# Late-stage second layers as seven products of halves (Strassen), summed over six experts in PSUM

## The chip, the cores and the metric

One core of a Trainium2 chip runs the whole program. The metric is the device time of one execution in microseconds (us), the median of several runs. Engines are named as in the profile: PE (TensorE matmuls), PEld (its weight loads), DVE (VectorE), ACT (ScalarE), POOL (GpSimd), SP (SyncE, which here only issues DMAs).

## The reference, cut to what matters

Eight batches of eight heads go through attention over a sliding window of 128 positions. Its output, 4608 tokens of 512 features, is the input of a mixture of eight experts. Every token goes through every expert; `P` only weighs the results.

```
x = attention(q, k, v)            # 4608 x 512
logits = x @ w_gate               # 4608 x 8
P = exp(logits - logits.max())
for _ in range(8):                # row and column normalisation in turn
    P /= P.sum(1, keepdims=True) + 1e-09
    P /= P.sum(0, keepdims=True) + 1e-09
    P *= N / E
for e in range(8):
    h = maximum(x @ w1[e], 0)     # 512 -> 1024
    out += P[:, e:e+1] * (h @ w2[e])   # 1024 -> 512
```

## The kernel before, in words

Instructions are issued in the order in which the code names them, and each engine works through its own list in that order. The 4608 tokens are 36 blocks of 128. `xT` holds the transposed attention output of all blocks on chip, in fp16.

**A unit** (`unit_atoms`, L92) is one expert on four blocks (512 tokens). Its first layer is eight atoms `l1`, each four matmuls with 512 moving columns (L103) and a ReLU on ACT that writes `hT` (L110). Its second layer is four atoms `l2`, one for each block, each eight matmuls (L116) that accumulate 128 tokens x 512 features in a PSUM bank. Whenever a weight tile of 128x128 is used, one weight load precedes the matmul. `woven` (L129) alternates the first layer of a unit with the second layer of the unit before.

**Experts 0 and 1** run while attention is going on. Class `Filler` (L148) hands out their atoms, budgeted by two estimates (`L1_US`, `L2_US`), so that PE has work while attention waits for ACT and DVE, and later while DVE does the eight normalisation rounds (L617 to L643). What is left over runs at L644. `P` is not known yet, so `keep` (L480) puts the raw results away: expert 0's into an fp32 accumulator `acc` on chip (L486), expert 1's into an fp16 tile `yo` with three buffers (L489), which `store` sends to the DRAM tensor `ysp` from ACT's queue (L478) when the next result is kept.

**Experts 2 to 7**, the late stage, start when the filler is empty. Expert by expert, the nine units of 512 tokens run, all in `woven`. `add` (L656) lets DVE multiply each result by its column of `P` and add it to `acc` (L667); with expert 2, it first scales expert 0's part (L660) and adds expert 1's from `yb` (L663), which `load_y` brings back. With expert 7 the block is sent out by SP. Weights come by POOL's queue, cast from fp32 to fp16 on the way, into two buffers each (L85, L87): expert e+1's load is issued at the first unit of expert e and waits until the buffer of expert e-1 is free. POOL has nothing else to do after attention.

PSUM has eight banks: two for the scores (`psS`), two buffers `psV` and four buffers `pmm`, which the atoms share. The tiles of attention lie in the pool `asb`, which stays open to the end.

Of the kernel before, what the change touches and what calls it, by code (L numbers as in the profile page):

```python
# [9 lines left out]
FP16 = mybir.dt.float16  # L10
FP32 = mybir.dt.float32
# [3 lines left out]
def kernel(  # L15
# [42 lines left out]
    ident_h = nc.inline_tensor(np.eye(P, dtype=np.float16), name="ident_c")  # L58
    ident32_h = nc.inline_tensor(np.eye(P, dtype=np.float32), name="ident32_c")

    ysp = nc.dram_tensor("ysp", [NBLK, P, HD], FP16, kind="Internal").ap()

    ctx.enter_context(tc.manual_schedule())
    per = ctx.enter_context(tc.tile_pool(name="per", bufs=1))
# [15 lines left out]
    def load_weights(e: int, first: int = 0, last: int = 2):  # L80
# [4 lines left out]
            nc.gpsimd.dma_start(out=w1ts[e], in_=moe_w1[e].rearrange("(dt p) f -> p dt f", p=P))  # L85
        if first <= 1 < last:
            nc.gpsimd.dma_start(out=w2ts[e], in_=moe_w2[e].rearrange("(ft p) d -> p ft d", p=P))  # L87

    acc: dict = {}


    def unit_atoms(e, b0, nb, pool, tag, bufs, finish):  # L92
# [49 lines left out]
            yield 0, a  # L142

    L1_US, L2_US = 0.87, 1.74
    XPE = 3
    CAST_AT = ((0, 1, 2, 3), (1, 2, 3, 4))

    class Filler:  # L148
# [49 lines left out]
                done += got  # L198
            return done

    with (
        tc.tile_pool(name="asb", bufs=1) as asb,
        tc.tile_pool(name="aps", bufs=1, space=bass.MemoryType.PSUM) as aps,
    ):
        mask = asb.tile([P, H, 2 * P], FP16, name="mask")
        rel = asb.tile([P, HD], FP16, name="rel", tag="yo", bufs=3)[:, 0 : 2 * P]

        def make_mask(u):
            for y in range(4 * u, 4 * u + 4):
# [17 lines left out]
            tails[b] = t32  # L227

        def load_qk(b):
            q32 = per.tile([P, H, RI * Dh], FP32, name=f"q32_{b}", tag="a8", bufs=9)  # L230
            k32 = per.tile([P, H, RI * Dh], FP32, name=f"k32_{b}", tag="a8", bufs=9)
            for t, src in ((q32, q), (k32, k)):
                nc.sync.dma_start(
                    out=t, in_=src[b, :, 0:SM, :].rearrange("h (p i) d -> p h (i d)", i=RI)
                )
            raw[b] = (q32, k32)

        def cast_qk(b, j):

            if j == 0:  # L240
                c16s[b] = per.tile([P, 2, RI, H, Dh], FP16, name=f"c16_{b}", tag="a8", bufs=9)
            for n in (1, 0):
                src = raw[b][n][:, 2 * j : 2 * j + 2, :].rearrange("p h (i d) -> p i h d", i=RI)
                to = c16s[b][:, n, :, 2 * j : 2 * j + 2, :]
                if n == 0:
                    nc.vector.tensor_copy(out=to, in_=src)
                else:
                    nc.scalar.copy(out=to, in_=src)  # L248
            if j == NDT - 1:
                raw.pop(b)  # L250
# [6 lines left out]

        def turn_qk(b):
            c16 = c16s.pop(b)
            qk = per.tile([P, 2, RI, NDT, P], FP16, name=f"qk_{b}", tag="a8", bufs=9)  # L260
            for n in range(2):
                nc.sync.dma_start(
                    out=qk[:, n].rearrange("p i j r -> p (i j) r"),
                    in_=c16[:, n].rearrange("p i h d -> p (i h d)"),
                    transpose=True,
                )
            KT[b] = qk
            homes(b)
# [12 lines left out]
            nc.sync.dma_start(out=QKT[b][2], in_=t16, transpose=True)  # L281

        def load_first():
            q32 = per.tile([P, H, RI * Dh], FP32, name="q32_0", tag="a8", bufs=9)
            k32 = per.tile([P, H, RI * Dh], FP32, name="k32_0", tag="a8", bufs=9)
            raw[0] = (q32, k32)
            for j in range(NDT):
                for n in (1, 0):
                    nc.sync.dma_start(
                        out=raw[0][n][:, 2 * j : 2 * j + 2, :],  # L290
                        in_=(q, k)[n][0, 2 * j : 2 * j + 2, 0:SM, :].rearrange(
                            "h (p i) d -> p h (i d)", i=RI
                        ),
                    )
                if j == 1:
                    load_v(0)
            load_v(1)
            load_tail(0)
            load_v(2)
            load_v(3)  # L300
            load_v(4)
            homes(0)
# [101 lines left out]
        def values(b, kb, u):  # L404

            nk, _ = sizes(kb)
            if u == 0:
                xsbs[b, kb] = asb.tile([P, H, Dh], FP16, name=f"xsb_{b}_{kb}", tag="xsb", bufs=3)
            psN = aps.tile([P, 4, Dh + 1], FP32, name=f"psN_{b}_{kb}_{u}", tag="psV", bufs=2)
            ops = []  # L410
            for y in range(2):
                for hb in range(2):
                    hh = 2 * y + hb
                    if kb > 0:
                        ops.append((hh, pts[b, kb - 1, u][:, 2 * hb + y, P : P + nk], vs[b, kb - 1][:, 4 * u + hh, 0 : Dh + 1]))
                    ops.append((hh, pts[b, kb, u][0:nk, 2 * hb + y, 0:nk], vs[b, kb][0:nk, 4 * u + hh, 0 : Dh + 1]))
            if kb == NKB - 1:
                ops = ops[0::2] + ops[1::2]
            for i, (hh, lhsT, rhs) in enumerate(ops):
                nc.tensor.matmul(  # L420
                    out=psN[0:nk, hh, :],
                    lhsT=lhsT,
                    rhs=rhs,
                    start=(i == 0),
                    stop=(i == len(ops) - 1),
                )
            if kb > 0:
                pts.pop((b, kb - 1, u))
            rden = asb.tile([P, 4], FP32, name=f"rden_{b}_{kb}_{u}", tag="rden", bufs=2)
            nc.vector.reciprocal(out=rden[0:nk, :], in_=psN[0:nk, :, Dh])  # L430
            nc.vector.tensor_tensor(  # L431
                out=xsbs[b, kb][0:nk, 4 * u : 4 * u + 4, :],
                in0=psN[0:nk, :, 0:Dh],
                in1=rden[0:nk, :].unsqueeze(2).to_broadcast([nk, 4, Dh]),
                op=ALU.mult,
            )
# [37 lines left out]

        def store():
            while stores:
                blk, yo = stores.pop(0)
                nc.scalar.dma_start(out=ysp[blk], in_=yo)  # L478

        def keep(e, blk, ps):  # L480
            store()
            if e == 0:
                g = blk // 4
                if g not in acc:
                    acc[g] = per.tile([P, 4, HD], FP32, name=f"acc_{g}", tag="a8", bufs=9)
                nc.vector.tensor_copy(out=acc[g][:, blk % 4, :], in_=ps)  # L486
            else:
                yo = asb.tile([P, HD], FP16, name=f"yo_{blk}", tag="yo", bufs=3)
                nc.vector.tensor_copy(out=yo, in_=ps)  # L489
                stores.append((blk, yo))  # L490

        spans = [(0, 2), (2, 2)] + [(4 * g, 4) for g in range(1, NG)]
        order = [(0, 0), (0, 1)]
# [40 lines left out]
        for n, (b, kb, u) in enumerate(steps):  # L534
# [63 lines left out]
            if b < B - 1 and at == (1 if b > 1 else 5) and b:  # L598
                load_tail(b + 1)
        filler.ready = 4 * B  # L600
        filler.fill(1.8)
        gates(4 * B - 4, NBLK)
        filler.ready = NBLK
# [1 line left out]

        nc.vector.tensor_reduce(out=mx_sb[:, 0:1], in_=L_sb, axis=AX.XY, op=ALU.max)
        filler.fill(1.0)
        psM = aps.tile([P, P], FP32, name="psM", tag="psV", bufs=2)
        nc.tensor.transpose(psM[0:1, :], mx_sb[:, 0:1], ident32)
        nc.vector.tensor_reduce(out=mx_sb[0:1, 1:2], in_=psM[0:1, :], axis=AX.X, op=ALU.max, negate=True)  # L610
        filler.fill(1.0)
        psM2 = aps.tile([P, 1], FP32, name="psM2", tag="psV", bufs=2)
        nc.tensor.matmul(out=psM2, lhsT=ones32[0:1, :], rhs=mx_sb[0:1, 1:2])
        nc.vector.tensor_copy(out=mx_sb[:, 2:3], in_=psM2)
        nc.scalar.activation(out=P_sb, in_=L_sb, func=AF.Exp, bias=mx_sb[:, 2:3])
# [1 line left out]
        for it in range(8):  # L617
# [10 lines left out]
                out=cs_sb, in_=P_sb.rearrange("p c e -> p e c"), axis=AX.X, op=ALU.add  # L628
            )
            filler.fill(2.9)  # L630
            psC = aps.tile([P, E], FP32, name=f"psC_{it}", tag="psV", bufs=2)
            nc.tensor.matmul(out=psC, lhsT=ones32, rhs=cs_sb)  # L632
            nc.vector.tensor_scalar(out=ca_sb, in0=psC, scalar1=1e-9, scalar2=None, op0=ALU.add)
            nc.vector.reciprocal(out=ca_sb, in_=ca_sb)
# [6 lines left out]
                op1=ALU.mult,  # L641
            )
            filler.fill(0.8)  # L643
        while filler.fill(5.0):  # L644
            pass
        store()
        load_weights(2)


        yb: dict = {}  # L650

        def load_y(g):
            yb[g] = asb.tile([P, 4, HD], FP16, name=f"yb_{g}", tag=("qN", "kN")[g % 2], bufs=2)
            nc.sync.dma_start(out=yb[g], in_=ysp[4 * g : 4 * g + 4].rearrange("m p d -> p m d"))

        def add(e, blk, ps):  # L656
            g = blk // 4
            a = acc[g][:, blk % 4, :]
            if e == 2:
                nc.vector.tensor_scalar(  # L660
                    out=a, in0=a, scalar1=P_sb[:, blk, 0:1], scalar2=None, op0=ALU.mult
                )
                nc.vector.scalar_tensor_tensor(  # L663
                    out=a, in0=yb[g][:, blk % 4, :], scalar=P_sb[:, blk, 1:2], in1=a,
                    op0=ALU.mult, op1=ALU.add,
                )
            nc.vector.scalar_tensor_tensor(  # L667
                out=a, in0=ps, scalar=P_sb[:, blk, e : e + 1], in1=a, op0=ALU.mult, op1=ALU.add
            )
            if e == E - 1:  # L670
                if blk < 4 * B:
                    t0 = S * (blk // 4) + P * (blk % 4)
                    nc.sync.dma_start(out=out[t0 : t0 + P, :], in_=a)
# [2 lines left out]
                        t0 = S * (2 * (blk - 4 * B) + half) + SM  # L676
                        nc.sync.dma_start(out=out[t0 : t0 + TL, :], in_=a[TL * half : TL * half + TL])

        def late():
            for e in range(2, E):  # L680
                for g in range(NG):
                    if g == 0 and e + 1 < E:
                        load_weights(e + 1)
                    if e == 2:
                        load_y(g)
                    yield 0, unit_atoms(e, 4 * g, 4, aps, ("pmm", "pmm"), (4, 4), add)

        for _, atom in woven(late()):
            atom()


# [28 lines left out]
```

## Time and profile before

| what | us |
|---|---|
| median of 3 runs (lowest, highest) | 1109.33 (1108.95, 1110.06) |
| the profiled execution, whole | 1111.33 |
| its span, first to last instruction | 1109.1 |
| PE busy in the span | 1079.8 |
| DVE, ACT, POOL busy | 404.7, 437.4, 70.2 |
| late stage, first matmul to last (354.0 to 1104.4) | 750.4 |

The mean granted TensorE clock is 0.996 of full speed. A group line of the page names source line, engine, operation, the tiles written and read, the shape and the count; after the bar stand the busy time and the mean duration of one, then the idle time of the engine just before these instructions with what ended it. Durations of matmuls overlap, so the pace is read from start to start. A timeline line gives the start, the time until the group's end, engine, line, operation and count, and in brackets the idle time before it. `POOLq`, `ACTq` and `SPq` lines are the issue of DMAs.

### The profile page before, as it was taken

Reading aid. Unit: us, or ns where it says so; the run is one execution under the profiler, and the core shown is the slowest. Engines: PE = TensorE matmul, PEld = TensorE weight load, DVE = VectorE, ACT = ScalarE, POOL = GpSimd, SP = SyncE. Lnnn points to the kernel's source line nnn. Section 1 sums busy time; section 2 is a strip of 40 time slices with the busy share of each in tenths; the row PEclk is TensorE's granted clock in tenths of the full one; section 3 lists DMA queues with packets and bytes.
Section 4 is the critical chain, followed back from the end, with each engine's and each line's share of the span. In section 5 each row is a group of like instructions: output and inputs, shape, how many; then the busy total and the mean of one; then the engine's idle time right before and its main releaser. Section 6 shows DMA issues by size and latency. Waiting matters only on the chain.

```text
span 1109.1 us, 14385 instructions
## 1 busy us (share of the span) xinstructions
PE 1079.8 (97%) x5963; PEld 505.1 (46%) x5963; DVE 404.7 (36%) x755; ACT 437.4 (39%) x729; POOL 70.2 (6%) x126
## 2 busy tenths in 40 slices
PE   5899999999999999999999999999999999999998
PEld 3564444444444444444444444444444444444443
DVE  4555666565482455542222222222222222222222
ACT  5566555555332433333333333333333333333332
POOL 2112133230000000000000000000000000000000
PEclk9999999999999999999999999999999999999999
DMA  9995598951326211040002200040002200001113
GB/s 205 199 239 139 110 194 172 191 122 41 108 41 123 47 39 38 1 76 1 1 1 38 38 1 1 1 77 1 1 1 38 38 1 1 1 20 76 77 76 95
DMA packets 127280, 73.90 MB, mean 67 GB/s; under 512 B 84464, under 2 KB 118512, under 8 KB 127216
## 3 DMA queue, kind: packets, MB, share of 16 engines
q1 hardware_dynamic: 108528, 51.33, 18.8%
q0 software_dynamic: 13072, 16.79, 9.6%
q10 hardware_dynamic: 5616, 4.88, 1.6%
q8 instruction: 46, 0.75, 0.3%
q14 instruction: 18, 0.15, 0.0%
HBM read 66.76 MB, written 14.16 MB: 73 GB/s over the span
## 4 chain that ended last, share of the span: by engine, by line
PE 84%; DVE 1%; DMA 1%; issue 0%; DVEq 0%
PE psh L103 41%; PE psy L116 41%; PE psN L420 1%; PE psS L372 1%; DMA ysp<-yo 1%; PE psG L464 0%; DVE acc L486 0%; DVE cs_sb L627 0%; PE psC L632 0%; DVE L_sb L621 0%; DVE yo L489 0%; DVE rs_sb L618 0%; DVE rs_sb L620 0%; DVE L_sb L635 0%; DVE acc L667 0%
## 5 line engine op out<-in xcount | busy, mean ns | idle before, releaser
L110 ACT ACTIVATE hT<-psh 128x512 f16<-128x512 f32 (+1 forms) x592 | 345.4, 586 | 576.4 <-PE psh L103 563.7
L103 PE MATMUL psh<-xT,w1t 128*128 128x512 f16 (+1 forms) x2368 | 554.8, 376 | 2.7 <-DVE yo L489 2.4
L116 PE MATMUL psy<-w2t,hT 128*128 128x512 f16 x2304 | 542.6, 379 | 0.0
L667 DVE SCALAR_TENSOR_TENSOR acc<-psy,L_sb,acc 128x512 f32<-128x512 f32 x216 | 162.2, 751 | 541.3 <-PE psy L116 541.3
L103 PEld LDWEIGHTS <-w1t 128*128 128x128 f16 x2368 | 226.8, 99 | 255.9 <-issue 9.1
L116 PEld LDWEIGHTS <-hT 128*128 128x128 f16 x2304 | 222.2, 98 | 264.8 <-issue 3.0
L385 ACT ACTIVATE pt<-psS 128x1024 f16<-128x1024 f32 (+2 forms) x80 | 68.0, 850 | 64.3 <-PE psS L372 41.5
L398 DVE TENSOR_TENSOR pt<-pt,mask 128x1024 f16<-128x1024 f16 (+2 forms) x80 | 53.2, 666 | 42.1 <-ACT pt L385 41.8
L489 DVE CAST yo<-psy 128x512 f16<-128x512 f32 x36 | 24.9, 691 | 47.7 <-PE psy L116 41.1
L420 PEld LDWEIGHTS <-pt 128*128 128x128 f16 (+2 forms) x576 | 29.2, 103 | 23.0 <-issue 7.2
L85 POOL DMA_DIRECT2D w1t<-in_moe_w_dram x8 | 6.1, 767 | 520.6 <-PE psh L103 520.6
L486 DVE COPY acc<-psy 128x512 f32<-128x512 f32 x36 | 24.8, 690 | 36.7 <-PE psy L116 36.6
L346 POOL CAST v<-v 128x512 f16<-128x512 f32 (+1 forms) x40 | 28.9, 723 | 128.1 <-DMA v<-in_v_dram 92.9
L420 PE MATMUL psN<-v,pt 128*128 128x65 f16 (+2 forms) x576 | 34.8, 199 | 0.9 <-DVE pt L398 0.7
L431 DVE TENSOR_TENSOR xsb<-psN,rden 128x256 f16<-128x256 f32 (+1 forms) x80 | 33.8, 423 | 3.0
L372 PE MATMUL psS<-qN,kN 64*128 64x256 f16 (+1 forms) x256 | 25.9, 274 | 3.9 <-ACT pt L385 3.0
L663 DVE SCALAR_TENSOR_TENSOR acc<-yb,L_sb,acc 128x512 f32<-128x512 f16 x36 | 27.0, 751 | 1.3
L273 POOL COPY kN<-qk 128x512 f16<-128x512 f16 x20 | 22.8, 1183 | 68.2 <-DMA qk<-c 68.2
L248 ACT CAST c<-k 128x512 f16<-128x512 f32 x32 | 19.5, 615 | 9.6 <-DMA k<-in_k_dram 3.8
L372 PEld LDWEIGHTS <-kN 64*128 64x128 f16 x256 | 9.2, 95 | 21.7 <-issue 19.4
L313 PE MATMUL psT<-ident,c 128*128 128x128 f16 x96 | 9.0, 249 | 10.1 <-ACT c L248 9.7
L660 DVE TENSOR_SCALAR acc<-acc,L_sb 128x512 f32<-128x512 f32 x36 | 17.2, 477 | 0.0
(48 smaller groups left out, 161.7 us busy)
## 6 DMA issues: line engine op xcount, KB each, us to landing
v<-in_v_dram SPq DMA_DIRECT2D x32, 256.0 KB, 4.1
w1t<-in_moe_w_dram POOLq DMA_DIRECT2D x8, 1024.0 KB, 8.2
w2t<-in_moe_w_dram POOLq DMA_DIRECT2D x8, 1024.0 KB, 9.1
out_dram<-acc SPq DMA_DIRECT2D x32, 256.0 KB, 2.0
q<-in_q_dram SPq DMA_DIRECT2D x7, 1024.0 KB, 7.0
k<-in_k_dram SPq DMA_DIRECT2D x7, 1024.0 KB, 8.9
ysp<-yo ACTq DMA_DIRECT2D x36, 128.0 KB, 2.1
yb<-ysp SPq DMA_DIRECT2D x9, 512.0 KB, 4.0
```

What stands on the lines that cost most here:

```text
L103: nc.tensor.matmul(out=ps[:, 0:nt], lhsT=w1ts[e][:, dt, P * ft : P * ft + P], rhs=xT[:, b0 : b0 + nb, dt, :], start=(dt == 0), stop=(dt == ...
L110: nc.scalar.activation(out=st["hT"][:, ft, 0:nt], in_=ps[:, 0:nt], func=AF.Relu)
L116: nc.tensor.matmul(out=ps, lhsT=st["hT"][:, ft, P * ms : P * ms + P], rhs=w2ts[e][:, ft, :], start=(ft == 0), stop=(ft == NFT - 1),)
L346: nc.gpsimd.tensor_copy(out=vt[0:nk, :, 0:Dh], in_=v32s.pop((b, kb))[0:nk])
L372: nc.tensor.matmul(out=ps[0:nk, hb, y, 0:n], lhsT=cols(b, 1, j, hb, kb), rhs=cols(b, 0, j, hb, kb, 1 + both),)
L385: nc.scalar.activation(out=pt[0:nk, :, 0 : nk + nn], in_=ps[0:nk, :, :, 0 : nk + nn].rearrange("p a y n -> p (a y) n"), func=AF.Exp, scale ...
L398: nc.vector.tensor_tensor(out=pt[0:nk, :, 0:w], in0=pt[0:nk, :, 0:w], in1=mask[0:nk, hs, 0:w], op=ALU.mult)
L420: nc.tensor.matmul(out=psN[0:nk, hh, :], lhsT=lhsT, rhs=rhs, start=(i == 0), stop=(i == len(ops) - 1),)
L431: nc.vector.tensor_tensor(out=xsbs[b, kb][0:nk, 4 * u : 4 * u + 4, :], in0=psN[0:nk, :, 0:Dh], in1=rden[0:nk, :].unsqueeze(2).to_broadcast ...
L489: nc.vector.tensor_copy(out=yo, in_=ps)
L663: nc.vector.scalar_tensor_tensor(out=a, in0=yb[g][:, blk % 4, :], scalar=P_sb[:, blk, 1:2], in1=a, op0=ALU.mult, op1=ALU.add,)
L667: nc.vector.scalar_tensor_tensor(out=a, in0=ps, scalar=P_sb[:, blk, e : e + 1], in1=a, op0=ALU.mult, op1=ALU.add)
```

## The change

The late stage is rewritten; attention and the first two experts' matmuls are as before.

1. Expert 0's results go to `ysp` too, as fp16, like expert 1's. `acc` of all tokens is gone.
2. After attention the pool `asb` is closed. In its place a pool `lp` holds experts 2 to 6: first-layer weights, the four quarters of the second-layer weights, and five sums or differences of quarters for each (`sums_of`), made by POOL. Expert 7 uses the old weight buffers. Each is loaded once, experts 2 to 6 in five DMAs each (before: two).
3. After the normalisation `P` is transposed by PE, written to DRAM (`ptd`) and read back for each unit, spread over all partitions (`load_p`).
4. A late unit is now 256 tokens and one expert; the order is token group by token group (18), in each the six experts. DVE multiplies `xT` by `P` ahead of the first layer (`make_x`): `P` is positive, so it may go through the ReLU.
5. The second layer has 256 tokens in two halves of 128, 1024 hidden in two halves, 512 features in two halves. Instead of eight products of halves there are seven, each four matmuls of 256 moving columns, from sums of halves of `h` (`make_sums`, DVE) and of weights. All seven are summed over the six experts in PSUM (three and a half banks), and `gather` combines them once per group into `acc`, which `begin` has filled with experts 0 and 1.

The core of the diff:

```diff
+        first_pool.close()
...
+        def load_last(e):
...
+            if e < E - 1:
+                W1L[e] = lp.tile([P, NDT, Fd], FP16, name=f"w1l_{e}")
+                bd = lp.tile([P, 2, NF2, HB], FP16, name=f"w2d_{e}")
+                st = lp.tile([P, 2, NF2, HB], FP16, name=f"w2s_{e}", tag="s4", bufs=2)
...
+                nc.gpsimd.dma_start(out=W1L[e], in_=w1src)
+                for to, (a, c) in ((q11, (0, 0)), (q12, (0, 1)), (q21, (1, 0)), (q22, (1, 1))):
+                    nc.gpsimd.dma_start(out=to, in_=src[a, c])
...
+        def sums_of(e, f6, f7, f4, f3, f1):
...
+                nc.gpsimd.tensor_tensor(out=to, in0=q[x], in1=q[y], op=op)
...
+        load_last(2)
+        load_last(3)
+        for e in range(2, E - 1):
+            sum_last(e)
+            if e + 2 < E - 1:
+                load_last(e + 2)
...
+        PT = 12
+        for c in range(NBLK // PT):
...
+            store()
+            pt_sb = per.tile([P, 2 * P], FP32, name=f"pt_sb_{c}", tag="yo", bufs=YO)
+            nc.vector.tensor_copy(out=pt_sb[0 : PT * E, 0:P], in_=psP[0 : PT * E, 0:P])
+            nc.sync.dma_start(
...
+            filler.fill(0.8)
...
+        units = [(g, e) for g in range(NBLK // 2) for e in range(2, E)]
...
+        def make_x(n):
...
+            nc.vector.tensor_tensor(
+                out=xs(n).rearrange("p (d b t) -> p d b t", d=NDT, b=2),
+                in0=xT[:, 2 * g : 2 * g + 2].rearrange("p b d t -> p d b t"),
+                in1=pbc.pop(n).unsqueeze(1).to_broadcast([P, NDT, 2, P]),
+                op=ALU.mult,
+            )
...
+        def l1_bank(n, i):
...
+            for f in range(2):
+                ft = 2 * i + f
+                for dt in range(NDT):
+                    nc.tensor.matmul(
...
+            nc.scalar.activation(out=h[n][:, 2 * i : 2 * i + 2, :], in_=ps, func=AF.Relu)
...
+        def product(n, m):
...
+            for f in range(NF2):
+                nc.tensor.matmul(
+                    out=Ms[g, bank][:, half, :],
+                    lhsT=left(n, m, f),
+                    rhs=W2L[e][RIGHT[m]][:, f, :],
...
+        store()
+        for n in range(2):
+            load_p(n)
+        filler.fill(3.0)
+        for n in range(2):
+            make_x(n)
+        while filler.fill(5.0):
+            pass
+        store()
+        load_last(E - 1)
+        sum_last(E - 1)
...
+        pairs = ((3, 4), (5, 2), (6, 7), (1,))
+        late: list = []
+        for n in range(len(units) + 1):
+            last = n > 0 and units[n - 1][1] == E - 1
+            if n > 0:
+                make_sums(n - 1)
+            for g, m in late:
+                gather(g, m)
...
+            if n > 0:
+                make_x(n + 1)
+                load_p(n + YO)
...
+            for i in range(4):
+                if n < len(units):
+                    l1_bank(n, i)
+                if n > 0:
+                    for m in pairs[i]:
+                        product(n - 1, m)
+                if last and i in (1, 2):
+                    for m in pairs[i - 1]:
+                        gather(units[n - 1][0], m)
```

`make_sums` is three DVE operations on fp16: two of 1024 elements a partition (sums over the hidden halves, differences over the token halves) and one of 512. `gather` is three DVE operations of 512 and six of 256 elements a group, each with a PSUM operand. `begin` is four operations of 512. The tag `yo` (three buffers) now serves the stored results of both experts, the transposed `P` and the tiles of `load_p`.

## The prediction

> **What bounds the kernel now.** I read the page's busy shares and chain first, then the groups by shape, then the timeline around the two places the change touches.
>
> ```profile
> PE 1079.8 (97%) x5963; PEld 505.1 (46%) x5963; DVE 404.7 (36%) x755; ACT 437.4 (39%) x729; POOL 70.2 (6%) x126
> ...
> PE psh L103 41%; PE psy L116 41%; PE psN L420 1%; PE psS L372 1%; DMA ysp<-yo 1%; PE psG L464 0%; DVE acc L486 0%; DVE cs_sb L627 0%; PE psC L632 0%; DVE L_sb L621 0%; DVE yo L489 0%; DVE rs_sb L618 0%; DVE rs_sb L620 0%; DVE L_sb L635 0%; DVE acc L667 0%
> ```
>
> The chain that ended last is expert matmuls (82%). The windows view shows how pure the late stage is:
>
> ```profile
> 366.00:700.00 334.00, 334.00 (x1550) 151.41 (x1548) 112.14 (x166) 115.85 (x194) 3.27 (x4) 1.00 0.11 21
> 700.00:1100.00 400.00, 400.00 (x1855) 181.38 (x1854) 87.86 (x117) 137.34 (x230) 3.27 (x4) 1.00 0.12 32
> ```
>
> Columns: stretch, length, then PE, PEld, DVE, ACT, POOL busy with counts, clock, DMA. PE never pauses, at 334/1550 = 215.5 ns per matmul of 512 columns; DVE is at 22 to 34%, POOL idle. Only fewer PE columns can shorten this stage. It lasts from 354.0 to the last matmul's end at 1104.4: 750.4 us, of which 3456 x 215.6 ns = 745.1 is pace and about 5 a stall at 357 to 362, shown below.
>
> **What the change takes away.** A unit of 256 tokens has 32 first-layer matmuls and 7 x 4 = 28 second-layer ones, each of 256 columns with a weight load of its own; 108 units make 6480. Before, the same work is 64 such halves. The price of the new shape is in the trace, from the first units of two blocks:
>
> ```profile
> 39.88 3.67 PE L103 MATMUL psh<-xT,w1t 128*128 128x256 f16 x32
> 43.39 3.62 PE L116 MATMUL psy<-w2t,hT 128*128 128x512 f16 x16
> ```
>
> 32 matmuls of 256 columns take 43.39 - 39.88 = 3.51 us, 109.7 ns each, though each has a weight load (98 ns median): the load still hides. 6480 x 109.7 = 710.8 us, so the stage loses 750.4 - 710.8 = **39.6 us**. Ends: half of 216 ns (108.0) gives 50.6; 112 ns gives 24.6.
>
> **Does the new stage keep PE fed?** One unit is 60 x 109.7 = 6.58 us. ACT: four ReLUs of 512 elements at 597 ns, 2.4 us. DVE: fp16 products of 1024 elements from SBUF (L398) take 0.68 us, 768 take 0.56, so `make_sums` is 0.68 + 0.68 + about 0.42 = 1.8; `make_x` of 1024 elements with an fp32 operand lies between 2 x 0.48 (L660, 512) and 2 x 0.75 (L663), I take the latter, 1.5, as L663 too has two operands of two types. `begin`: 2 x (0.48 + 0.75) = 2.5. `gather`: 3 x 0.75 (L667) + 6 x 0.42 (L431, 256) = 4.8. A group of six units costs DVE 6 x 3.3 + 2.5 + 4.8 = 27 us of 39.5. It must also be in time: the last ReLU of a unit ends some 0.4 us into the next, the sums by 2.2; the products that need them come 2.6, 4.4 and 6.1 us in. At a group's turn, the gathers of products 5 and 2 end near 0.4 us into the next unit and free the scores' banks, which are wanted at 0.9. If the sums ran at one element per cycle (twice 0.68), the gathers would be some 1.5 us later and PE would wait about 1 us at each of 18 turns. I take 0; end 18.
> SP issues 108 reads of `P`, three units (20 us) ahead; 128 KB stores land in 1.7 to 8.5 us, so they are early.
>
> **What the change adds at the start of the stage: the term that decides.** POOL must load and add for experts 2 to 6 after attention gives its memory back (last mask use 286.4, last transpose of `xsb` about 294; I take 290), and all six experts are wanted within the first six units, where before expert 3 was wanted 125 us after expert 2. The parts:
> - An issue by POOL is 0.75 us (L85). Ten for experts 2 and 3: 7.7.
> - 1 MB lands 8.2 to 9.1 us after issue, and two back to back move at about 205 GB/s, 5.1 us each. Expert 2 is there near 303.
> - An add of 1024 fp16 elements by POOL is not in the trace. A POOL cast of 512 takes 0.61 us (L346 median), a strided copy of 512 takes 1.07 (L273 median). Ends: 1.2 (1024 at the cast's rate) and 4.3 (two operands at the copy's rate). I take 2.4, two operands at the cast's rate, the plain-stride row being the nearer.
> - POOL and DVE hold each other up. These are DVE's and POOL's timelines:
>
> ```profile
> 171.33 0.98 DVE L398 TENSOR_TENSOR pt<-pt,mask 128x768 f16<-128x768 f16 x1 [0.65 <-ACT pt L385]
> ...
> 174.28 1.41 DVE L398 TENSOR_TENSOR pt<-pt,mask 128x768 f16<-128x768 f16 x1 [0.43 <-ACT pt L385]
> ...
> 276.20 0.56 DVE L398 TENSOR_TENSOR pt<-pt,mask 128x768 f16<-128x768 f16 x1 [0.66 <-ACT pt L385]
> ```
>
> ```profile
> 170.81 4.46 POOL L273 COPY kN<-qk 128x512 f16<-128x512 f16 x4 [10.73 <-DMA qk<-c]
> ```
>
> The same product takes 0.56 us alone and up to 1.41 under POOL's copies; POOL's copies stretch from 1.07 to 1.44 at most. So I put 0.5 us on each add: 2.9.
> Chain: 303 + 25 adds x 2.9 (72.5) + 15 issues x 0.77 (11.6) = 387. Expert 7's two loads are issued behind them and land at 402; its five adds end at 417. PE, without stalls, would begin the stage at 354, want expert 7's first layer at 354 + 5 x 6.58 = 387, its sums from 394, and finish that step at 400. It finishes at about 418: **18 us late**. Each 0.1 us on an add moves this by 3 us.
> PE's own way there has little slack left, so part is paid twice over, by two things. DVE's two-operand work in the normalisation rounds (L621, L635, 0.46 each) and in the first units waits behind adds. And the stores, twice as many, share the DMA engines with weight loads:
>
> ```profile
> 349.79 8.55 DMA ysp<-yo
> 358.33 0.03 issue
> 358.36 0.05 DVEq L489
> 358.41 0.04 issue
> 358.45 0.70 DVE yo L489
> 359.16 0.04 issue
> 359.20 7.89 PE psh L103 x28
> ```
>
> This is the chain view: beside one weight load a store takes 8.5 us (1.7 without), DVE's cast behind it waits for the buffer, ACT's queue waits for DVE with its ReLUs, and PE stops 2.4 us. Some 20 results leave in 287 to 354, and weights now move through all of it. With a result each 3.4 us and three buffers, 10.3 us cover 0.7 + 2 + 6, mostly. I give these together 13 us of PE's time ahead of the stage, covered by the 18, and **3 us** beyond it; ends 0 and 15. The way of `P` through DRAM (two landings of 2 to 8.5 us against about 10 us of filler) lies under the same cover.
>
> [...]
>
> **The end.** Behind the last matmul stood one 0.75 us step and the output. Now `gather` of the last group stands behind the last sums, 4.8 us of which about 3.6 come after PE: **+3 us**.
>
> **Sum.** 1109.1 - 39.6 + 18 + 3 + 3 = 1093.5 of span. The profiled execution took 2.2 us more than its span; the median of the runs, 1109.33, is 0.2 above the span, so the median after is forecast as **1094 us**.
>
> **The rivals.**
> - *The start is hidden* (adds at 1.2 to 2.2 us, or stores that don't bite): 1109.3 - 39.6 + 3 gives 1073, with a few us of stall 1080. For it: 60 us of filler lie between attention and the stage. Against: 25 adds and 15 loads in it. Chance 0.22.
> - *Slower: POOL's chain.* Same place, an add of 4.3 us: 30 x 1.4 = 42 us more, 1136. It decides from the point where the losses reach 39.6, an add of about 3.4 us with its waits. [...] Against: the operands here run in plain stride. Chance 0.17.
> - *PE stalls at every group's turn* because DVE is late: +18, or sums at half rate, about 1104 to 1112. Against: 12 us of slack a group. Chance 0.08.
> - *The shape does not pay*: a weight load per 109.7 ns could slip when both operands change source; at 116 ns the stage is as long as before. Against: the row of 32. Chance 0.03.
> - My forecast, 1084 to 1105: 0.50.
>
> The range leaves out the ends of the first two: 1072 to 1118. A measurement of this kernel can tell about 0.2% (2 us) from no change. Faster 0.77: forecast, hidden start, half of the late turns; within 0.2%: 0.05; slower 0.18.
>
> **What will show it.** Right: 60 matmuls per 6.6 us after about 420 us with PE full; idle PE between 330 and 420, ended by POOL's sums or expert 7's load; adds of 2.4 to 3 us. Wrong: idle PE in the later groups, ended by DVE, which would put the loss at 18 turns; a pace above 112 ns; or adds near 1.2 us, and then no idle time at 387.

## The result and the profile after

The changed kernel takes 1125.97 us (median of 4 runs, 1124.32 to 1126.65), the kernel before, measured beside it, 1109.32 (1108.95 to 1110.06): a ratio of 1.0147, 95% interval 1.0129 to 1.0165. It is slower by 1.5%, where 1094 was forecast. The profiled execution took 1126.23 us, its span is 1124.5, against 1109.1 before: **15.4 us** to account for.

The page after, busy shares and the chain that ended last:

```profile
PE 1052.0 (94%) x8990; PEld 805.5 (72%) x8990; DVE 653.7 (58%) x1136; ACT 437.8 (39%) x729; POOL 145.6 (13%) x171
...
PE 79%; DVE 5%; issue 1%; ACT 0%; DVEq 0%
```

PE has 27.8 us less to do, and the span grew all the same: PE's share fell from 97% to 94%, and 5% of the chain is now VectorE. The windows view says where. The first stretch runs from the end of attention to the start of the late stage, the other two lie in the late stage:

```profile
308.50:404.00 95.50, 67.26 (x311) 30.52 (x310) 71.37 (x89) 19.01 (x32) 72.47 (x51) 0.86 0.89 148
440.00:700.00 260.00, 260.00 (x2385) 233.03 (x2383) 150.91 (x244) 94.69 (x159) 0.00 (x0) 1.00 0.17 50
700.00:1100.00 400.00, 400.00 (x3667) 358.54 (x3665) 234.49 (x379) 145.90 (x245) 0.00 (x0) 1.00 0.16 47
```

The late stage is what the change promised: full, at 260/2385 = 109.0 ns per matmul of 256 columns, with VectorE at 58% and nothing lost at the groups' turns. The loss lies in front of it. By stage:

| stretch | before, us | after, us | difference |
|---|---|---|---|
| start to the last gate matmuls (end of attention) | 294.05 | 308.5 | +14.4 |
| from there to the first late matmul (354.04; 404.01) | 60.0 | 95.5 | +35.5 |
| late stage to its last matmul | 750.4 | 711.9 | -38.5 |
| after the last matmul | 4.7 | 8.6 | +3.9 |

**The second row: the normalisation rounds.** VectorE's timeline inside one long wait and after it:

```profile
352.06 0.47 DVE L685 SCALAR_TENSOR_TENSOR L_sb<-L_sb,ca_sb 128x288 f32<-128x288 f32 x1
352.56 0.45 DVE L668 TENSOR_REDUCE rs_sb<-L_sb 128x36 f32<-128x288 f32 x1
353.05 8.36 DVE L669 TENSOR_SCALAR rs_sb<-rs_sb 128x36 f32<-128x36 f32 x1
361.44 0.38 DVE L670 RECIPROCAL rs_sb<-rs_sb 128x36 f32<-128x36 f32 x1
361.85 1.90 DVE L671 TENSOR_TENSOR L_sb<-L_sb,rs_sb 128x288 f32<-128x288 f32 x1
```

and POOL's in the same time:

```profile
352.97 2.18 POOL L633 TENSOR_TENSOR w2f<-w2s,w2d 128x1024 f16<-128x1024 f16 x1
355.05 4.24 POOL L633 TENSOR_TENSOR w2f<-w2d,w2s 128x1024 f16<-128x1024 f16 x2
359.21 2.15 POOL L633 TENSOR_TENSOR w2f<-w2s,w2d 128x1024 f16<-128x1024 f16 x1
361.28 2.14 POOL L633 TENSOR_TENSOR w2f<-w2d 128x1024 f16<-128x1024 f16 x1
```

A step of 36 elements a partition, which takes 0.18 us in other rounds, is on record as *busy* for 8.36: it began 0.08 us after the first of five adds and ended when the fourth did. L671 (0.46 alone) then waits out the fifth. The record calls this time busy and not idle, so the waits view does not show it; it shows in durations only. PE sees the end of it:

```profile
350.99 0.59 PE L682 MATMUL psC<-cs_sb,ones 128*128 128x8 f32 x2 [8.35 <-DVE cs_sb L677]
364.50 0.60 PE L682 MATMUL psC<-cs_sb,ones 128*128 128x8 f32 x2 [7.98 <-DVE cs_sb L677]
378.60 0.60 PE L682 MATMUL psC<-cs_sb,ones 128*128 128x8 f32 x2 [8.49 <-DVE cs_sb L677]
```

A handy measure of the rounds, used for every run below, is the time from the first to the last weight load of the column-sum matmuls (L682; L632 before): 63.1 us (315.7 to 378.8), against 29.1 before (301.5 to 330.6). These are the lines, before and after:

```profile
L632 PEld LDWEIGHTS psC<-cs_sb,ones x16: 186/189/190, 301.5 to 330.6; 128*128 128x128 f32 x16
```

```profile
L682 PEld LDWEIGHTS psC<-cs_sb,ones x16: 186/238/333, 315.7 to 378.8; 128*128 128x128 f32 x16
```

In the whole stretch from 308.5 to 404.0 PE is idle for 28.2 us (before, from 294 to 354: 0.9). The other 8 us of the 35.5 are PE being busy longer, 67.3 us against 59.1 for about the same number of matmuls (311 and 309); the granted clock is 0.86 there, against 1.00.

**The first row: a pause at 47 us.** Windows of before, then of after (length, PE, PEld, DVE, ACT, POOL, clock, DMA share, GB/s):

```profile
47.00:58.00 11.00, 7.48 (x84) 5.20 (x81) 8.59 (x19) 7.11 (x10) 1.39 (x3) 0.90 0.98 166
58.00:72.00 14.00, 14.00 (x163) 9.95 (x160) 7.82 (x20) 8.91 (x20) 2.98 (x10) 0.96 1.01 268
```

```profile
47.00:58.00 11.00, 0.38 (x4) 0.31 (x4) 1.87 (x5) 1.50 (x3) 1.32 (x4) 0.67 1.04 189
58.00:72.00 14.00, 11.60 (x89) 7.62 (x89) 7.06 (x16) 7.87 (x13) 1.32 (x4) 0.53 1.03 276
```

PE stands for 11 us, and the granted clock is 0.53 in the 14 us behind. The DMA engines were full in both kernels (share 0.98 to 1.04). ACT's timeline names the odd thing:

```profile
55.83 0.33 ACTq L478 DMA_DIRECT2D ysp<-yo  x1
56.50 1.14 ACT L247 CAST c<-k 128x512 f16<-128x512 f32 x2 [12.37 <-DMA v<-in_v_dram]
```

ACT casts keys, but is released by a load of *values*, which it does not use. Ahead of the cast in its queue stands a store of expert 0's result, which the kernel before did not have. The trace names a completion counter for every DMA. Those that SP and ACT issue share eight (99, 101 to 105, 107 and 108; POOL's have 110 to 117), and after the first use of each, all 372 of them here were issued only when the last DMA with the same counter had landed. Expert 0's third store has the same one (99) as a load of values that SP issued at 43.86; that load lands at 55.75, beside expert 1's weights, and ACT issues the store at 55.83. That was the suspicion; the experiments test it.

**The small rest.** Expert 7's sums hold VectorE once more (L768 took 2.60 us, L737 3.13; the medians are 0.68 and 1.22), and PE once:

```profile
429.81 1.87 PE L753 MATMUL psh<-aux,w1l 128*128 128x256 f16 x8 [2.49 <-DVE aux L737]
```

and the last gathers, 2.73 and 1.54 us, end 3.2 us behind the last matmul instead of a step of 0.75.

### The profile page after: what moved, and what is told of

Same layout as the page of the kernel before. It is cut to its first block, busy times and chain, and to the rows that moved or that the text cites. A ratio compares the mean times of both kernels' runs of the same rounds, so it can differ in the third digit from the quotient of the medians.

```text
span 1124.5 us, 21205 instructions
## 1 busy us (share of the span) xinstructions
PE 1052.0 (94%) x8990; PEld 805.5 (72%) x8990; DVE 653.7 (58%) x1136; ACT 437.8 (39%) x729; POOL 145.6 (13%) x171
## 4 chain that ended last, share of the span: by engine, by line
PE 79%; DVE 5%; issue 1%; ACT 0%; DVEq 0%
PE psh L753 33%; PE psS_m L808 17%; PE psV_m L808 12%; PE psh L102 7%; PE psy L115 7%; DVE rs_sb L669 2%; PE psN L420 1%; PE psS L371 1%; DVE L_sb L671 1%; DVE acc L854 0%; DVE aux L737 0%; DVE L_sb L685 0%; DVE cs_sb L677 0%; PE psC L682 0%; DVE yo L483 0%
## 5 line engine op out<-in xcount | busy, mean ns | idle before, releaser
L760 ACT ACTIVATE hs<-psh 128x512 f16<-128x512 f32 x432 | 257.9, 597 | 457.1 <-PE psh L753 370.1
L753 PE MATMUL psh<-aux,w1l 128*128 128x256 f16 x2880 | 373.4, 273 | 2.5 <-DVE aux L737 2.5
L753 PEld LDWEIGHTS <-w1l 128*128 128x128 f16 x2880 | 282.1, 98 | 35.9 <-issue 2.7
L808 PEld LDWEIGHTS <-hs 128*128 128x128 f16 x2592 | 254.0, 98 | 30.1 <-DVE hs L765 0.4
L765 DVE TENSOR_TENSOR hs<-hs 128x1024 f16<-128x1024 f16 x108 | 74.9, 694 | 284.7 <-ACT hs L760 284.7
L102 PE MATMUL psh<-xT,w1t 128*128 128x512 f16 (+1 forms) x640 | 151.1, 375 | 0.4 <-ACT hT L109 0.3
L115 PE MATMUL psy<-w2t,hT 128*128 128x512 f16 x576 | 136.4, 382 | 0.0
L109 ACT ACTIVATE hT<-psh 128x512 f16<-128x512 f32 (+1 forms) x160 | 87.8, 555 | 121.2 <-PE psh L102 100.8
L737 DVE TENSOR_TENSOR aux<-xT,pbc 128x1024 f16<-128x1024 f16 x108 | 133.3, 1235 | 0.0
L115 PEld LDWEIGHTS <-hT 128*128 128x128 f16 x576 | 53.7, 99 | 62.4 <-issue 5.9
L102 PEld LDWEIGHTS <-w1t 128*128 128x128 f16 x640 | 58.9, 103 | 51.5 <-issue 10.6
L768 DVE TENSOR_TENSOR hs<-hs 128x1024 f16<-128x1024 f16 x108 | 75.9, 703 | 0.0
## 6 DMA issues: line engine op xcount, KB each, us to landing
k<-in_k_dram SPq DMA_DIRECT2D x7, 1024.0 KB, 10.3
```

The lines of the kernel that those rows point to most:

```text
L102: nc.tensor.matmul(out=ps[:, 0:nt], lhsT=w1ts[e][:, dt, P * ft : P * ft + P], rhs=xT[:, b0 : b0 + nb, dt, :], start=(dt == 0), stop=(dt == ...
L109: nc.scalar.activation(out=st["hT"][:, ft, 0:nt], in_=ps[:, 0:nt], func=AF.Relu)
L115: nc.tensor.matmul(out=ps, lhsT=st["hT"][:, ft, P * ms : P * ms + P], rhs=w2ts[e][:, ft, :], start=(ft == 0), stop=(ft == NFT - 1),)
L737: nc.vector.tensor_tensor(out=xs(n).rearrange("p (d b t) -> p d b t", d=NDT, b=2), in0=xT[:, 2 * g : 2 * g + 2].rearrange("p b d t -> p d ...
L753: nc.tensor.matmul(out=ps[:, f, :], lhsT=W1L[e][:, dt, P * ft : P * ft + P], rhs=xs(n)[:, HB * dt : HB * dt + HB], start=(dt == 0), stop=( ...
L760: nc.scalar.activation(out=h[n][:, 2 * i : 2 * i + 2, :], in_=ps, func=AF.Relu)
```

## The experiments

Ratios are to the kernel before, with 95% intervals.

| run | us | ratio | rounds, us |
|---|---|---|---|
| after | 1125.97 | 1.0147 [1.0129, 1.0165] | 63.1 |
| no_adds | 1092.62 | 0.9859 [0.9845, 0.9874] | 29.2 |
| before_adds | 1125.77 | 1.0159 [1.0144, 1.0174] | 43.2 |
| half_adds | 1137.9 | 1.0265 [1.0248, 1.0282] | 63.7 |
| gap_memset | 1126.64 | 1.0163 [1.0146, 1.018] | 63.4 |
| gap_dma | 1143.75 | 1.0315 [1.0298, 1.0331] | 82.2 |
| rounds_psum | 1100.75 | 0.9929 [0.9911, 0.9946] | 28.4 |
| dve_adds | 1092.04 | 0.9855 [0.984, 0.9869] | 29.2 |
| pool_store | 1133.41 | 1.0225 [1.021, 1.0241] | 63.5 |
| qk2_one_later | 1125.12 | 1.0152 [1.0137, 1.0167] | 62.9 |
| qk2_two_later | 1114.85 | 1.0057 [1.004, 1.0074] | 62.5 |
| dve_adds_qk2 | 1081.13 | 0.9761 [0.9738, 0.9783] | 29.1 |
| rounds_psum_qk2 | 1090.17 | 0.9843 [0.9817, 0.9869] | 28.4 |

### Are the adds the cause of the slow rounds?

Two causes are set against each other: VectorE's steps wait for POOL's adds (called the lock theory), or the loads and stores slow the stretch (traffic).

**no_adds**: the loads stay, the sums on POOL go.

```diff
-                nc.gpsimd.tensor_tensor(out=to, in0=q[x], in1=q[y], op=op)
...
+            q.update(f1=q["q11"], f3=q["q22"], f4=q["q11"], f6=q["q22"], f7=q["q11"])
```

> The 30 adds of weight quarters are left out (the products read quarters in place of sums), so part of the computation is missing; loads, stores and everything else stay. Lock theory: the eight normalisation rounds shrink from 66 us to about 35, because DVE's two-operand steps no longer wait for POOL; the late stage starts near 370 instead of 404 and has no pause near 429. Time 1083 to 1090 us. Traffic theory (the weight loads and the doubled stores slow the stretch, not the adds): the rounds stay above 55 us, time 1115 to 1126.

Measured: 1092.62 us; the rounds are back at 29.2 us with all loads beside them. Not the whole way to the 1083 to 1090 expected, since PE pauses in front of the late stage, where stores run beside weight loads:

```profile
358.71 1.13 PE L102 MATMUL psh<-xT,w1t 128*128 128x512 f16 x4 [4.18 <-DVE yo L483]
364.68 3.61 PE L102 MATMUL psh<-xT,w1t 128*128 128x512 f16 x16 [1.52 <-DVE yo L483]
```

The pause at 47 us is as in the kernel after: it has nothing to do with the adds.

**before_adds**: the kernel before, with 25 adds of the same size on POOL, on scratch tiles, and no other DMA.

```diff
         filler.ready = 4 * B
+        for n in range(25):
+            pt = asb.tile([P, 4, 2 * P], FP16, name=f"scratch_{n}", tag="pt", bufs=4)
+            nc.gpsimd.tensor_tensor(out=pt, in0=mask[:, 0:4, :], in1=mask[:, 4:8, :], op=ALU.add)
```

> The kernel before, with 25 POOL adds of 1024 fp16 elements on scratch data put in after attention, without any new DMA; the result is not touched. Lock theory: the adds alone stretch the normalisation rounds by 20 to 32 us, time 1129 to 1142 us. Traffic theory: nothing reads or writes the adds' data, POOL is idle there and no transfer is added, so 1109 to 1111.

Measured: 1125.77 us, 17.5 more than before. So adds alone slow the rounds, to 43.2 us, and the time. But it is 3.2 us below the range expected, and each wait is here of one add at most, though 25 stand back to back:

```profile
299.42 1.71 DVE L622 TENSOR_SCALAR rs_sb<-rs_sb 128x36 f32<-128x36 f32 x1
...
312.39 2.13 DVE L638 SCALAR_TENSOR_TENSOR L_sb<-L_sb,ca_sb 128x288 f32<-128x288 f32 x1
```

### How long does VectorE wait?

**half_adds**: each add is made as two of half the size.

```diff
-                nc.gpsimd.tensor_tensor(out=to, in0=q[x], in1=q[y], op=op)
+                for lo in range(0, NF2, 2):
+                    nc.gpsimd.tensor_tensor(
+                        out=to[:, lo : lo + 2], in0=q[x][:, lo : lo + 2], in1=q[y][:, lo : lo + 2], op=op
+                    )
```

> Each POOL add is cut into two of 512 elements: the same work in twice as many instructions. If DVE is kept out for a number of POOL instructions (four in the trace, 8.4 us), its long waits halve to some 4.3 us and the rounds shorten by 10 to 15 us: time 1110 to 1117. If it is kept out until POOL has nothing ready, the long waits stay near 8.4 us or more and the time is 1124 to 1132. If each instruction were a fair turn, waits would be at most 1.2 us and the time near 1100.

Measured: 1137.9, more than any theory had. Adds of 1.1 us, and still VectorE waits like this:

```profile
354.05 9.39 DVE L674 TENSOR_TENSOR L_sb<-L_sb,rs_sb 128x288 f32<-128x288 f32 x1
```

Eight half adds long, as long as four whole ones before. It is not a number of instructions that VectorE waits for. The rounds took 63.7 us as in after; the 12 us more lie just behind the part that this measures, at the adds of the last expert, where VectorE's last step of the rounds waited for all ten half adds and PE stood idle 10.48 us for it:

```profile
380.32 11.67 DVE L688 SCALAR_TENSOR_TENSOR L_sb<-L_sb,ca_sb 128x288 f32<-128x288 f32 x1
```

**gap_memset** and **gap_dma**: something else between the adds, a small fill or one of the loads that stood behind them. In gap_dma the four loads of quarters are also issued in another order.

```diff
                 nc.gpsimd.tensor_tensor(out=to, in0=q[x], in1=q[y], op=op)
+                if e < E - 1:
+                    nc.gpsimd.memset(gap, 0.0)
```

```diff
-            sum_last(e)
-            if e + 2 < E - 1:
-                load_last(e + 2)
+            sum_last(e, load_last(e + 2, False) if e + 2 < E - 1 else ())
...
                 nc.gpsimd.tensor_tensor(out=to, in0=q[x], in1=q[y], op=op)
+                if between:
+                    between.pop(0)()
```

> The kernel after, with a fill of 128x2 elements on GpSimd behind each sum, which reads no tile. [...]

> The kernel after, with the loads of the expert two later issued one by one between the sums on GpSimd, instead of five loads behind five sums. VectorE was let in before the fifth sum in every case so far where loads followed it. Theory that only back-to-back sums shut VectorE out: its long waits shrink from 8.4 us to one sum (about 2.2 us) or two, the rounds take 40 to 52 us instead of 66, and the time falls by 12 to 24 us, to 1102 to 1114. [...]

Measured: 1126.64 and 1143.75. Fills change nothing (1125.97 in after); the longest waits are 6.16, 8.24 and 8.25 us. With the loads in between it got worse, not better: waits of 6.31, 6.04 and 6.66 us through two adds and the loads between them, and then one of 24.55. VectorE's and POOL's timelines of gap_dma:

```profile
361.42 24.55 DVE L675 TENSOR_TENSOR L_sb<-L_sb,rs_sb 128x288 f32<-128x288 f32 x1
```

```profile
362.02 2.13 POOL L637 TENSOR_TENSOR w2f<-w2d 128x1024 f16<-128x1024 f16 x1
364.08 0.79 POOL L615 DMA_DIRECT2D w2s<-in_moe_w_dram  x1
364.89 2.13 POOL L637 TENSOR_TENSOR w2f<-w2s,w2d 128x1024 f16<-128x1024 f16 x1
...
383.54 2.10 POOL L637 TENSOR_TENSOR w2f<-w2d 128x1024 f16<-128x1024 f16 x1
```

One step of 0.46 us stood through eleven adds. By the record it began 0.6 us ahead of the first of them, while POOL issued a load, and the 0.8 us in which POOL issued the next one (364.08) did not let it in either. What does end such a wait stays open: between one add (before_adds) and eleven (gap_dma) everything was seen.

### Which steps of VectorE wait?

Over all these runs the steps of the rounds that wait are L669, L671 and L685 by the lines of after (0.18, 0.46 and 0.46 us alone; up to 8.38 in after, 24.55 in gap_dma and 11.67 in half_adds), and in the late stage the fp16 sums and products (up to 2.60 and 3.13 in after); never a reduction (0.43 to 0.68 us in the rounds), a reciprocal (0.20 and 0.38), or a step that reads PSUM (L683, also a scaling by a constant, takes 0.15 to 0.17 us throughout). All that waited read SBUF alone, with two tensors, or scale SBUF to SBUF.

**rounds_psum**: the matrix of the rounds and its row sums lie in PSUM, the adds stay on POOL. (The column sums' PSUM tile moves to another pool to make room.)

```diff
+        R = aps.tile([P, GT], FP32, name="psR", tag="psV", bufs=2)
+        Pr = R[:, 0 : NBLK * E].rearrange("p (c e) -> p c e", e=E)
+        rs = R[:, 320 : 320 + NBLK]
...
-            nc.vector.tensor_scalar(out=rs_sb, in0=rs_sb, scalar1=1e-9, scalar2=None, op0=ALU.add)
+            nc.vector.tensor_scalar(out=rs_sb, in0=rs, scalar1=1e-9, scalar2=None, op0=ALU.add)
...
-                out=P_sb,
-                in0=P_sb,
+                out=Pr,
+                in0=Pr,
```

> The kernel after, with the matrix of the normalisation rounds held in PSUM instead of SBUF: VectorE's three steps that were seen to wait (scaling the row sums, and the two products with the broadcast sums) read their first operand from PSUM. GpSimd's sums stay where they are. In all runs so far only these steps waited, while reductions, reciprocals and the copies out of PSUM never did. Theory that a step waits only if both of its tensor operands, or its source and target, are in SBUF: the waits vanish, the rounds take 30 to 38 us instead of 66, the late stage starts some 30 us earlier, and the time is 1092 to 1100 us. Rival, any two-operand step of VectorE waits for GpSimd's sums wherever its operands are: the waits of 8 us stay and the time is 1120 to 1130.

Measured: 1100.75 us, a hair above the range, and no step of the rounds waits, beside the same adds (POOL adds from 339.02 to 349.4 in this run):

```profile
342.25 0.47 DVE L688 SCALAR_TENSOR_TENSOR psR<-psR,ca_sb 128x288 f32<-128x288 f32 x1
...
343.25 0.20 DVE L672 TENSOR_SCALAR rs_sb<-psR 128x36 f32<-128x36 f32 x1
...
343.89 0.47 DVE L674 TENSOR_TENSOR psR<-psR,rs_sb 128x288 f32<-128x288 f32 x1
...
345.84 0.46 DVE L688 SCALAR_TENSOR_TENSOR L_sb<-psR,ca_sb 128x288 f32<-128x288 f32 x1
```

The place of the operand that is read decided here: L672 and the last L688 write to SBUF and did not wait either (0.20 and 0.46 us). The rest to 1092 is PE waiting 3.13 and 2.53 us for stores' buffers before the late stage, and 2.53 and 2.40 us for products of VectorE behind the adds of experts 6 and 7.

**dve_adds**: VectorE makes the sums itself, experts 2 and 3 after the rounds, 4 before the late loop, 5 to 7 in its first steps.

```diff
-                nc.gpsimd.tensor_tensor(out=to, in0=q[x], in1=q[y], op=op)
+                nc.vector.tensor_tensor(out=to, in0=q[x], in1=q[y], op=op)
...
-        for e in range(2, E - 1):
-            sum_last(e)
-            if e + 2 < E - 1:
-                load_last(e + 2)
...
+        for e in (2, 3):
+            sum_last(e)
+            load_last(e + 2)
+            filler.fill(0.8)
```

> The kernel after, with all sums of weights on VectorE: experts 2 and 3 after the normalisation, expert 4 before the late loop, 5 to 7 within its first steps; the loads stay on GpSimd's queue and in the same number. Lock theory: without a two-operand operation on GpSimd the rounds take 34 to 38 us as in no_adds, the late stage starts at 370 to 385, some 5 to 10 us of sums come onto VectorE's path, and the time is 1090 to 1103 us. Rival, the loads themselves slow the rounds, or VectorE's sums are as dear as GpSimd's (2.2 us each, 66 us in all on the path of the late stage's first steps): 1115 or more.

Measured: 1092.04 us, rounds 29.2, first late matmul at 371.9. An add costs VectorE 0.68 us, a third of POOL's 2.1 (timeline of dve_adds_qk2, below):

```profile
340.37 0.68 DVE L633 TENSOR_TENSOR w2f<-w2s,w2d 128x1024 f16<-128x1024 f16 x1
340.97 1.28 DVE L633 TENSOR_TENSOR w2f<-w2d,w2s 128x1024 f16<-128x1024 f16 x2
```

### What is the pause at 47 us?

**pool_store**: the first four of expert 0's stores from POOL's queue, whose DMAs have other counters than those eight (110 to 117 in after).

```diff
-                nc.scalar.dma_start(out=ysp[e, blk], in_=yo)
+                (nc.gpsimd if e == 0 and blk < 4 else nc.scalar).dma_start(out=ysp[e, blk], in_=yo)
```

> The first four stores of expert 0 are issued by POOL instead of ACT. Theory: in the changed kernel ACT's third store waits 11 us for a completion counter that it shares with a load of v, and ACT's copies and so PE wait behind it (47 to 58 us); with the stores off ACT's queue that pause goes, and attention ends about 13 us earlier, time 1110 to 1115 us. Rival: the pause is the DMA engines, full with expert 1's weights and the next loads; then it stays or moves, time 1122 to 1127.

A miss: 1133.41 us, and the pause is longer. The timelines of POOL and PE:

```profile
55.60 0.61 POOL L345 CAST v<-v 128x512 f16<-128x512 f32 x1 [11.66 <-DMA v<-in_v_dram]
...
57.46 1.66 POOL L478 DMA_DIRECT2D ysp<-yo  x3
```

```profile
64.39 1.44 PE L312 MATMUL psT<-ident,c 128*128 128x128 f16 x12 [16.55 <-DVE yo L483]
```

In POOL's queue the stores stood behind casts of those same values. The move exchanged one wait for the load by another and says nothing for or against the counter.

**qk2_one_later** and **qk2_two_later**: the loads of batch 2's queries and keys, which number two among the eight, are issued later. The first leaves the third store on the counter of the late load, the second puts it on that of a load of values that landed at 39.56.

```diff
-            if (b, at) == (0, 7):
+            if (b, at) == (1, 0):
                 load_qk(2)
```

```diff
-            if (b, at) == (0, 7):
+            if (b, at) == (1, 1):
                 load_qk(2)
```

> The kernel after, with the load of batch 2's queries and keys issued three steps of attention later (at the first step of batch 1 instead of step 7 of batch 0). In the program this leaves the completion counter of expert 0's third store as it is: the counter of the load of values that lands at 55.8 us. It is the control for qk2_two_later. Counter theory: the pause of TensorE between 47 and 58 us stays, and the time is 1123 to 1128 us. Rival, traffic: the third store and the loads of values are late because the load of the queries and keys shares the DMA engines with expert 1's weights; with it moved away the pause shrinks, and the time falls by 5 to 14 us, to 1112 to 1121.

> The same load one step later still (second step of batch 1). Expert 0's third store now shares its completion counter with a load of values two earlier, which landed at about 40 us, before the store is wanted. Nothing else differs from qk2_one_later but one step's place of two loads. Counter theory: the pause between 47 and 58 us is gone (at most 3 us of it left), attention ends near 296 us instead of 308, and the time falls by 10 to 14 us, to 1111 to 1116. Rival, traffic: as qk2_one_later, within 3 us. The rounds of the normalisation, with GpSimd's sums beside them, keep their 66 us in both theories.

Measured: 1125.12 and 1114.85 us. One step's place of two loads is worth 10.3 us. PE in the windows of the one and of the other:

```profile
47.00:58.00 11.00, 0.00 (x0) 0.10 (x1) 1.39 (x3) 1.11 (x3) 1.07 (x3) 0.62 1.08 193
```

```profile
47.00:58.00 11.00, 7.82 (x80) 5.22 (x79) 7.73 (x18) 7.26 (x11) 1.12 (x2) 0.80 1.09 197
58.00:72.00 14.00, 14.00 (x155) 9.57 (x153) 7.00 (x18) 7.82 (x18) 3.01 (x9) 0.91 0.95 277
```

DMA is as full in both (share 1.08 and 1.09). And the load of values on counter 99 lands no earlier in qk2_two_later, at 56.37 (55.75 in after, 56.13 in qk2_one_later). But there the third store has another counter, and ACT's queue goes on without it:

```profile
45.14 0.33 ACTq L478 DMA_DIRECT2D ysp<-yo  x1
45.82 1.14 ACT L247 CAST c<-k 128x512 f16<-128x512 f32 x2 [2.05 <-DVE c L245]
```

So it was the counter, not the traffic. The last gate matmul starts at 298.0, 3.0 later than before (295.0), 11.3 earlier than after (309.3). What makes the 3.0 stays open.

### Both repairs

**dve_adds_qk2** and **rounds_psum_qk2** join the second move with each cure of the rounds.

> Both repairs together: sums on VectorE and the load of batch 2's queries and keys at the second step of batch 1. If the two losses are separate (the startup's pause by the counter, the slow rounds by GpSimd's sums), the gains add: dve_adds less 10 to 14 us, that is 1078 to 1092 us, under the kernel before. Rival: the pause's time comes back as a later wait (weights not landed when the late stage starts), and the time is that of dve_adds less at most 4.

> The rounds in PSUM and the load of batch 2's queries and keys at the second step of batch 1. If the two gains add, rounds_psum less 10 to 12 us, 1081 to 1090; against dve_adds_qk2 (1081) it has no sums on VectorE but the pause at expert 7's sums (some 3 us). If the rounds still wait: 1109 to 1117.

Measured: 1081.13 and 1090.17 us. The gains add (1092.04 - 10.9; 1100.75 - 10.6), the second with 0.2 us over the range expected. The first beats the kernel before by 2.4%:

```profile
PE 1041.9 (96%) x8990; PEld 799.1 (74%) x8990; DVE 631.6 (58%) x1166; ACT 436.4 (40%) x729; POOL 81.0 (7%) x141
```

Its late stage starts at 360.9, 6.9 us later than before (354.04).

## Why the prediction was wrong, by its own steps

- *The late stage loses 39.6 us*: right. It lost 38.5; the pace was a little better than 109.7 ns, and the stretch of expert 7's sums took the difference back.
- *PE stays fed*: right, with VectorE at 58% and full PE from 433 us on.
- *Adds of 2.4 us*: right, 2.11 to 2.36 for the 25 of experts 2 to 6.
- *POOL's chain, 18 us*: the right end by luck, two errors that cancelled. The sums of expert 6 ended at 388.45, forecast 387; but the first began at 323.86, not 303, and 25 adds with their issues took 65 us, not 84. The 0.5 us put on each add for its time beside VectorE was on the wrong engine: POOL's adds hardly stretched (2.36 us at most of those 25), VectorE did the waiting (8.53 at most). Expert 7's second load then waited for the filler's last second layer (issued at 404.48), which the forecast had at 402 on chip. All this cost PE only some 5 us (6480 matmuls at 109.0 ns are 706 us, the stage took 711.9), because PE was not there sooner.
- **"I give these together 13 us of PE's time ahead of the stage, covered by the 18"**: the step that failed, in size and in cover. From the end of attention to the late stage PE lost 35.5 us, some 34 of it in the rounds. No sum stands behind the 13. The one size shown was a row in which a product took 0.85 us more beside POOL's copies; I took the wait to be at most one operation of the other engine, an estimate that no row of before showed. In before_adds, where no wait is longer than one add (2.13 us), the rounds grew by 14.1 us; in the changed kernel the wait was four adds and more (8.53 us), in gap_dma eleven (24.55). I also listed only the products (L621, L635) as steps that can wait; two of the three longest waits (8.36 and 8.38 us) are in the scaling of the row sums, L619 before and L669 after. And it was not covered: the rounds are one dependent chain, so all of it went on PE's path, and POOL's chain, which was to cover it, ended before PE arrived.
- **"attention and the first two experts' matmuls are as before"**, in the change's description, and no term for it in the sum: 14.4 us. I had counted the doubled stores only where weight loads for the late stage move, not at the start of the program, where one of them has the counter of a load that lands at 55.75, and ACT's queue stands behind it for 12.37 us. With the store moved off that counter, 11.3 of the 14.4 came back.
- *The end, 3 us*: 3.9.
- The slower rival named the right place, POOL's adds, but set its price by POOL's time per add (3.4 us and up). The adds were at 2.1, and it was slower nevertheless. The sign to watch for, idle PE between 330 and 420, was there, ended by VectorE's column sums and not, as said, by POOL's sums.

## What to carry to other kernels

Work that went to an idle GpSimd was not free here, as VectorE had a chain of dependent small steps in the same time (up to 8.53 us for one of 0.46): look for VectorE steps whose *duration* is many times that of their kin, and either put one operand in PSUM (rounds 63.1 to 28.4 us) or let VectorE do the work (0.68 us an add instead of 2.1). A DMA added to ACT's queue made ACT wait 12.37 us for a transfer it had nothing to do with, since the two had one completion counter; ask of each new DMA which one before it has the same counter, when that lands, and what is queued behind it. Where a sum holds two delays to lie under each other's cover, ask whether they are on the same engine's chain.

## What the runs showed of the hardware

- VectorE's products, sums and scalings that read SBUF alone took up to 24.55 us (gap_dma) beside GpSimd's adds, where 0.18 to 0.46 us is usual in the rounds; reductions (0.43 to 0.68 us), reciprocals (0.20 and 0.38) and steps that read PSUM (0.15 to 0.47) did not wait in any of these runs. An issue of a load between two adds (0.79 us) did not end a wait in gap_dma. What does was not found.
- Holding an operand in PSUM cost nothing: 0.47 us against 0.46 for 288 fp32 elements.
- An fp16 add of 1024 elements a partition took 0.68 us on VectorE and 2.1 on GpSimd.
- After PE's pause of 11 us, the granted clock was 0.53 in the next 14 us (0.96 in the kernel before, without the pause).
